# Windowed attention and a gated FFN on one core: queries and keys of steps 4 to 7 in other tiles, and a remade order

## The chip, the core and the metric

The kernel runs on one NeuronCore of a Trainium2 chip. Its engines are TensorE (PE: matmuls; PEld is its weight load), VectorE (DVE), ScalarE (ACT), GpSimd (POOL) and SyncE (SP, which issues the DMAs). The metric is the device time of one execution in microseconds (us).

## The reference

The inputs are q, k and v of 4 batches, 8 heads, 768 tokens and 64 features, 8 memory tokens per head, and the weights of an FFN (512 to 1024 to 512) that come in float64. All heads of one token, side by side, are a row of 512 numbers.

```
for each chunk c of 32 tokens:                       # 24 chunks
    k_full = concat(mem_k, k[16 before .. 8 after])  # 8 + 56 rows
    v_full = concat(mem_v, v[the same])
    a = softmax(q_c @ k_full.T / 8)
    out[c] = a @ v_full
x = out, heads side by side                          # 4 x 768 x 512
h = relu(x @ w_in)                                   # 4 x 768 x 1024
conv = w0 * h[t-1] + w1 * h[t] + w2 * h[t+1]         # per feature, zeros outside
result = (h * sigmoid(conv)) @ w_out                 # 4 x 768 x 512
```

## The kernel before

**Steps of attention.** There are 32 steps, eight to a batch (NU = 8): two halves of 384 tokens (`hf`), in each four pairs of heads (`cc`). A step loads a tile of queries `q_d` (128x768), of keys `k_t` (128x504) and of values `v_t` (128x768), 384, 252 and 384 KB. Its work, with the names that the profile shows:

- the scores `s` (L481), 12 small matmuls of half-size tiles, which the profile counts as 24;
- softmax without the division: the row maximum `top` (L397, DVE), then by the step's letter in `SOFT` either a subtraction on DVE (L402) and one exponential on ACT (L435), or six to seven exponentials on ACT (L423); the row sum `z` (L448), a tiny addition to it (L452, DVE or POOL by `ZADD`), its reciprocal (L455), and the normalisation of `e` (L459, DVE or POOL by `NORM`);
- three transposes `t` (L502), copied to `a_d` by ACT (L513);
- the values' product `a` (L521), 12 small matmuls of half-size tiles, counted as 24;
- the result as two parts whose sum is exact: `x_hi` (L530, ACT) and `x_lo` (L533, DVE).

**FFN.** Each product of the FFN is three matmuls, hi by hi, hi by lo and lo by hi, which the prediction calls a group. The first (L556) makes a tile `f` of 128 features by 384 tokens from four values of `cc`; relu (L573) writes it to `h`. A gate is a first tap (L583 on ACT, L587 on DVE, by `TAP`), two more taps (L593, DVE), a sigmoid (L597) and a product (L601, DVE or POOL, by `MULT`), then a split in two parts (L611 ACT, L614 DVE or POOL, by `LO`). The second product (L632) goes to the output by `o_sb` (L644, ACT) and a DMA. The weights are read as float64 words, 512 KB a piece, eight pieces for each product, and turned into hi and lo in `from_f64` (L286 to L363), with a choice of engines for each piece by a letter of `W_IN` and `W_OUT`. PSUM has two banks for `s`, one each for `t` and `a`, and four for `f`.

**What sets the order.** Nothing runs where it is written. Each operation is given to a `Plan` with an engine, a cost, a due time and its tiles, and `Plan.run` then emits all of them: on each engine it picks among those that could start first the one with the lowest due time. The due times are straight lines in the table `DUE` (start, slope). A matmul operation names a mode, half tiles ("tiled") or whole ones ("whole"), and a change of mode has a cost in the plan. The order that comes out is fixed for each engine when the program is built; on the chip an engine waits at its next instruction until its inputs are there. All loads go through one queue of SP, in order.

**Where the changed tiles lie.** Steps 0 to 3 have queries and keys in the eight tiles of `h`, later used for the relu outputs of batches 1 to 3; all other steps share two `q_d` and two `k_t`. The ring `g` of 16 tiles holds the relu outputs of batch 0 and then the gated splits.

Of the kernel before, what the change touches and what calls it, by code (L numbers as in the profile page):

```python
# [19 lines left out]
CH, LEFT, RIGHT, NMEM = 32, 16, 8, 8  # L20
# [3 lines left out]
NC = 12  # L24
NG = NC // 4
KC = STEP * (NC - 1) + KW
# [3 lines left out]
WC = 512  # L30


W_IN, W_OUT = "CRScCmcc", "McCCMcmm"

TAP = "AAAAAAAAAAAAAAVVAAAAAAAAAVVVVAAA"
MULT = "VVVGGGGGGVGGGGGGGGVGGVGVVGGGGVVV"
LO = "VGVVVVVGGVVVVVGGVVVGGGGVVVGGVVVV"
SOFT = "VVAVVVVVVVABABAAAVVVVVABBBVVAVAB"  # L40
NORM = "GGGGGGGGVVGGGGGGGGGGGGGGVGVVVGVV"
ZADD = "VGGGGVGGGGGVGGVGGVVVVGGGVGGVVVVV"
GROUP = "11111111"

DUE = {
    "early": (1.3, 2.83), "qk0": (-13.5, 0.8), "v0": (104.5, 0), "late": (-19.1, 0), "w_in": (-14.7, 2.93),
    "w_in_load": (-18.2, 4.91), "w_out": (78.5, 2.37), "w_out_load": (4.1, 15.21), "load": (-130.9, 0),
# [4 lines left out]
    "gate": (29.9, 2.03)  # L52
}


# [7 lines left out]
class Plan:  # L63
# [47 lines left out]
    def run(self):  # L111
        ops = self.ops
        n = len(ops)
# [21 lines left out]
        for _ in range(n):  # L135
            best = None
            for e, c in cand.items():
# [20 lines left out]
                if not at:  # L158
                    continue
                t0 = min(at)[0]  # L160
                i = min(
                    (ops[i][2] + (SWITCH if ops[i][7] and ops[i][7] != table else 0) + (MODE if ops[i][8] and ops[i][8] != mode else 0), i)
                    for t, i in at
                    if t <= t0 + 1
                )[1]
# [4 lines left out]
            t, e, i = best  # L170
            eng, cost, due, do, after, tiles, shared, tab, md, late = ops[i]
# [1 line left out]
                cost += 1283  # L173
                table = tab
            if md and md != mode:
                cost += 95 if md == "tiled" else 120
                mode = md
            if e == "DMA":
                queue_free = max(queue_free, t + 600) + cost
# [31 lines left out]


PAIRS = False
SWITCH, MODE = 100.2, 12.1


@with_exitstack
def attention_then_gated_ffn(
# [15 lines left out]
    P = 128  # L234
    NCC, NFC = DM // P, DFF // P
# [9 lines left out]
    def tile_of(tag, n, shape, dtype=F32, pool=None):  # L245

        plan.ring(tag, n)
        pool = pool or work
        return Tile(tag, lambda: pool.tile(shape, dtype, name=tag, tag=tag, bufs=n))

    def bank(tag, n):
        return tile_of(tag, n, [P, 512], pool=psum)
# [13 lines left out]
    def lin(name, i):  # L266
        return DUE[name][0] + DUE[name][1] * i
# [104 lines left out]
    def attention(steps, due, soft, norm, zadd):  # L372
# [9 lines left out]
        for i, n in enumerate(steps):  # L382
            b, r = divmod(n, NU)
            cc = r % NCC

            q_d, k_t = (tile_of(*(("h", NFC) if n < 4 else (x, 2)), y) for x, y in (("q_d", [P, NC, 2 * CH]), ("k_t", [P, KC])))
            v_of[n] = v_t = tile_of("v_t", 3, [P, NG, 2, 2, D])
            s = bank("s", 2)
            qk, vd = (lin("qk0", n), lin("v0", n)) if n < 4 else (due[i] - DUE["load"][0], due[i] - DUE["load"][0] + DUE["load"][1])
            load(q_d, q[b, hf, cc], qk, "p c q -> p (c q)")  # L390
            load(k_t, k[b, hf, cc], qk)
            load(v_t, v[b, hf, cc], vd, "p g c h d -> p (g c h d)")
# [6 lines left out]
            if soft == "V":  # L399
# [3 lines left out]
                        out=part(e, i), in0=s_(), in1=part(top, i).unsqueeze(2).broadcast_to([P, 2 * NG, KW]), op=ALU.subtract  # L403
                    ), (s, (top, i)), ((e, i),),
                )
            else:
# [3 lines left out]
                        out=part(top, i), in0=part(top, i), scalar1=-SCALE, scalar2=None, op0=ALU.mult  # L410
# [21 lines left out]
        due = due[-1]  # L432
# [23 lines left out]
        for i, n in enumerate(steps):  # L456
# [3 lines left out]
                    out=part(e, i), in0=part(e, i), in1=part(z, i).unsqueeze(2).broadcast_to([P, 2 * NG, KW]), op=ALU.mult  # L460
# [4 lines left out]
    def load(tile, src, due, flat=None):  # L465
        size = 1
        for x in src.shape:
            size *= x
        plan.op(
            "DMA", size * 4 / 400, due,  # L470
            lambda: nc.sync.dma_start(out=tile.t.rearrange(flat) if flat else tile.t, in_=src), w=(tile,),
        )
# [196 lines left out]
    def steps(i, n):  # L669

        while i < n:
            size = GROUP[i // 4] == "2" and i % 2 == 0 and 2 or 1
            attention(range(i, i + size), T_ATT[i : i + size], SOFT[i], NORM[i], ZADD[i])
            i += size

    def through_gate(b, fc, due, keep=False):
        i = b * NFC + fc
        return gate(fc, hs[b, fc][0], due, TAP[i], MULT[i], keep)

# [10 lines left out]
    g = []  # L690
    for fc in range(NFC):
        due = lin("gate0", fc)
        g.append(split(*through_gate(0, fc, due), due, LO[fc]))
    for fc in range(NFC):
# [5 lines left out]
    y = [through_gate(1, fc, lin("gate1", fc), True) for fc in range(NFC)]  # L700
    g = [split(*y[fc], lin("split1", fc), LO[NFC + fc]) for fc in range(NFC)]
    steps(16, 24)
# [10 lines left out]
    for b in range(2, B):  # L713
        tokens_in(b, (0, 1), t, 4.2)
        g = []
        for fc in range(NFC):
            due = t + lin("gate", fc)
            g.append(split(*through_gate(b, fc, due), due, LO[b * NFC + fc]))
        if b + 1 < B:
# [81 lines left out]
```

## Time and profile before

| | us |
|---|---|
| median of 3 runs | 359.25 |
| lowest and highest run | 357.82, 360.33 |
| the profiled execution, its own time | 359.63 |
| the span of its profile | 357.6 |
| busy PE, DVE, ACT, POOL | 341.4, 244.7, 240.4, 125.2 |

The profile is of one execution. Its span runs from the first instruction to the last; the execution's own time has some 2 us around it. Busy times of PE are modelled at their ends, since matmuls are pipelined; from one start to the next says more. A wait is put down to the event that came last.

### The profile page before, as it was taken

Reading aid. Unit: us, or ns where it says so; the run is one execution under the profiler, and the core shown is the slowest. Engines: PE = TensorE matmul, PEld = TensorE weight load, DVE = VectorE, ACT = ScalarE, POOL = GpSimd, SP = SyncE. Lnnn points to the kernel's source line nnn. Section 1 sums busy time; section 2 is a strip of 40 time slices with the busy share of each in tenths; the row PEclk is TensorE's granted clock in tenths of the full one; section 3 lists DMA queues with packets and bytes.
Section 4 is the critical chain, followed back from the end, with each engine's and each line's share of the span. In section 5 each row is a group of like instructions: output and inputs, shape, how many; then the busy total and the mean of one; then the engine's idle time right before and its main releaser. Section 6 shows DMA issues by size and latency. Waiting matters only on the chain.

```text
span 357.6 us, 7589 instructions
## 1 busy us (share of the span) xinstructions
PE 341.4 (95%) x3000; PEld 302.1 (84%) x3000; DVE 244.7 (68%) x408; ACT 240.4 (67%) x492; POOL 125.2 (35%) x167
## 2 busy tenths in 40 slices
PE   1699999999999999999999999999999999999996
PEld 1588899999899987778888899997878799998886
DVE  3899898988889998779933026889644128998000
ACT  4468588878679999887979158877466345675101
POOL 2376554442373253774572003354010002560000
PEclk9989999999999999999999999999999999999999
DMA  7999961969623146134416200006272000000111
GB/s 267 402 387 311 383 234 63 341 208 283 209 95 116 25 139 227 68 104 152 129 44 250 88 31 0 2 0 188 80 294 75 30 31 2 0 0 3 59 59 61
DMA packets 19909, 48.63 MB, mean 136 GB/s; under 512 B 2337, under 2 KB 6689, under 8 KB 19873
## 3 DMA queue, kind: packets, MB, share of 16 engines
q1 hardware_dynamic: 19872, 48.14, 39.0%
q8 instruction: 24, 0.39, 0.5%
q14 instruction: 13, 0.10, 0.1%
HBM read 41.84 MB, written 6.29 MB: 135 GB/s over the span
## 4 chain that ended last, share of the span: by engine, by line
PE 69%; DVE 10%; DMA 5%; ACT 5%; POOL 5%; issue 4%; SPq 1%; POOLq 0%; DVEq 0%; ACTq 0%
PE f L632 33%; PE f L556 24%; PE a L521 5%; PE s L481 5%; DVE c L593 3%; PE t L502 2%; DMA h<-in_k_dram 2%; POOL c L601 2%; DMA w<-in_w_out_dram 2%; ACT c L597 2%; DMA w<-in_w_in_dram 2%; POOL w_top L293 2%; DVE z L448 1%; DVE w_top L299 1%; DVE top L397 1%
## 5 line engine op out<-in xcount | busy, mean ns | idle before, releaser
L632 PE MATMUL f<-w_out_hi,g 128*128 128x512 f32 (+1 forms) x400 | 127.6, 391 | 0.2 <-ACT o_sb L644 0.2
L556 PE MATMUL f<-x_hi,w_in_hi 128*128 128x384 f32 x256 | 88.7, 346 | 0.0
L632 PEld LDWEIGHTS f<-w_out_hi,g 128*128 128x128 f32 x400 | 74.1, 188 | 16.3 <-ACT o_sb L644 0.4
L556 PE MATMUL f<-x_hi,w_in_lo 128*128 128x384 f32 x256 | 86.2, 337 | 0.1
L556 PE MATMUL f<-x_lo,w_in_hi 128*128 128x384 f32 x256 | 86.1, 336 | 0.0
L593 DVE SCALAR_TENSOR_TENSOR c<-h,cw,c 128x768 f32<-128x768 f32 x48 | 65.9, 1380 | 27.6 <-ACT c L583 26.1
L632 PE MATMUL f<-w_out_lo,g 128*128 128x512 f32 (+1 forms) x200 | 77.0, 385 | 0.0
L556 PEld LDWEIGHTS f<-x_hi,w_in_hi 128*128 128x128 f32 x256 | 48.1, 188 | 1.2
L556 PEld LDWEIGHTS f<-x_hi,w_in_lo 128*128 128x128 f32 x256 | 48.2, 188 | 0.5 <-POOL w_in_lo L358 0.4
L556 PEld LDWEIGHTS f<-x_lo,w_in_hi 128*128 128x128 f32 x256 | 48.1, 188 | 0.0
L632 PEld LDWEIGHTS f<-w_out_lo,g 128*128 128x128 f32 x200 | 37.6, 188 | 7.2
L601 POOL TENSOR_TENSOR c<-c,h 128x768 f32<-128x768 f32 x9 | 15.8, 1752 | 70.2 <-ACT c L597 68.1
L459 POOL TENSOR_TENSOR e<-e,z 128x384 f32<-128x384 f32 x24 | 24.9, 1035 | 41.4 <-DVE z L455 27.1
L644 ACT COPY o_sb<-f 128x512 f32<-128x512 f32 (+1 forms) x25 | 14.1, 569 | 35.1 <-PE f L632 32.8
L573 ACT ACTIVATE h<-f 128x384 f32<-128x384 f32 x48 | 23.1, 492 | 17.2 <-PE f L556 16.8
L521 PEld LDWEIGHTS a<-a_d,v_t 128*64 128x64 f32 x768 | 25.7, 140 | 10.3 <-issue 5.0
L513 ACT COPY a_d<-t 64x384 f32<-64x384 f32 x64 | 30.3, 474 | 4.3 <-PE t L502 3.3
L533 DVE TENSOR_TENSOR x_lo<-a,x_hi 128x384 fp32r<-128x384 f32 x32 | 17.6, 551 | 22.3 <-ACT x_hi L530 22.2
L521 PE MATMUL a<-a_d,v_t 128*64 128x64 f32 x768 | 29.9, 229 | 1.9 <-ACT a_d L513 1.8
L597 ACT ACTIVATE c<-c 128x768 f32<-128x768 f32 x32 | 26.9, 845 | 3.8 <-DVE c L593 3.6
L530 ACT CAST x_hi<-a 128x384 fp32r<-128x384 f32 x32 | 15.4, 481 | 20.2 <-PE a L521 18.6
L423 ACT ACTIVATE e<-s,top 128x64 f32<-128x64 f32 (+3 forms) x96 | 24.4, 319 | 4.2 <-DVE top L409 2.8
(73 smaller groups left out, 479.8 us busy)
## 6 DMA issues: line engine op xcount, KB each, us to landing
v_t<-in_v_dram SPq DMA_DIRECT2D x32, 384.0 KB, 4.1
q_d<-in_q_dram SPq DMA_DIRECT2D x28, 384.0 KB, 5.1
k_t<-in_k_dram SPq DMA_DIRECT2D x28, 252.0 KB, 5.2
out_dram<-o_sb SPq DMA_DIRECT2D x23, 256.0 KB, 2.1
w<-in_w_in_dram SPq DMA_DIRECT2D x8, 512.0 KB, 5.9
w<-in_w_out_dram SPq DMA_DIRECT2D x8, 512.0 KB, 6.4
h<-in_q_dram SPq DMA_DIRECT2D x4, 384.0 KB, 7.0
h<-in_k_dram SPq DMA_DIRECT2D x4, 252.0 KB, 7.1
```

The costliest lines, as they stand in the source:

```text
L423: nc.scalar.activation(part(e, i)[r, g, c], s_()[r, g, c], AF.Exp, bias=part(top, i)[r, g : g + 1], scale=SCALE, accum_out=part(z, i)[r, g ...
L459: lambda i=i: (nc.vector if norm == "V" else nc.gpsimd).tensor_tensor(out=part(e, i), in0=part(e, i), in1=part(z, i).unsqueeze(2).broadcas ...
L481: nc.tensor.matmul(s.t[j * D : (j + 1) * D, o : o + KW], lhsT=q_d.t[:, c], rhs=k_t.t[:, c * STEP : c * STEP + KW], start=True, stop=True,)
L513: nc.scalar.copy(out=a_d[r, :, p, :], in_=t.t[r, : NG * P].rearrange("p (g q) -> p g q", q=CH))
L521: nc.tensor.matmul(a.t[h * D : (h + 1) * D, g * P + j * D : g * P + (j + 1) * D], lhsT=v_t.t[:, g, j, h], rhs=a_d[:, 4 * g + 2 * j + h].re ...
L533: lambda: nc.vector.tensor_tensor(out=x_lo.t[:, cc], in0=a.t[:, :TW], in1=x_hi.t[:, cc].bitcast(F32), op=ALU.subtract),
L556: nc.tensor.matmul(f.t[:, :TW], lhsT=w_in_p[c][:, fc, cc], rhs=x_p[a].t[:, cc], start=(cc == 0 and i == 0), stop=(cc == NCC - 1 and i == 2),)
L573: nc.scalar.activation(h.t[:, 1 + o : 1 + o + TW], f.t[:, :TW], AF.Relu)
L593: lambda i=i: nc.vector.scalar_tensor_tensor(out=c.t, in0=h.t[:, i : i + S], scalar=w[i], in1=c.t, op0=ALU.mult, op1=ALU.add), (*H, c), (c ...
L597: plan.op("A", act(S), due, lambda: nc.scalar.activation(c.t, c.t, AF.Sigmoid), (c,), (c,), table="sigmoid")
L601: lambda: (nc.vector if mult == "V" else nc.gpsimd).tensor_tensor(out=y(), in0=c.t, in1=h.t[:, 1 : S + 1], op=ALU.mult), (c, h), (h if kee ...
L632: nc.tensor.matmul(ps.t[:, :n], lhsT=g[fc][a].t[:, tt * P : (tt + 1) * P], rhs=w_out_p[c][:, fc, o : o + n], start=(fc == 0 and i == 0), s ...
```

## The change

Queries and keys of steps 4 to 7 go into tiles of the ring `g` (16 tiles) instead of the two `q_d` and two `k_t`, and their loads, and those of the values of these steps, get due times of the lines `qk0` and `v0`, as steps 0 to 3 have. In the plan the change from half tiles to whole ones is counted as 200 ns instead of 120. The tables of due times, of engines (`TAP`, `MULT`, `LO`, `SOFT`, `NORM`, `ZADD`) and of the weights' splits are other ones, and so is the order on every engine.

```diff
-W_IN, W_OUT = "CRScCmcc", "McCCMcmm"
+W_IN, W_OUT = "CRRcCmcS", "ScMMSMRS"
...
-NORM = "GGGGGGGGVVGGGGGGGGGGGGGGVGVVVGVV"
+NORM = "GGGGVGGGVVGGGGGGVVGVGGGVVVVVVVVV"
...
-    "early": (1.3, 2.83), "qk0": (-13.5, 0.8), "v0": (104.5, 0), "late": (-19.1, 0), "w_in": (-14.7, 2.93),
+    "early": (1.3, 2.45), "qk0": (-13.5, 0.48), "v0": (45, 1.91), "late": (-0.2, 2.08),
...
-                cost += 95 if md == "tiled" else 120
+                cost += 95 if md == "tiled" else 200
...
-SWITCH, MODE = 100.2, 12.1
+SWITCH, MODE = 110.1, 13.1
...
-            q_d, k_t = (tile_of(*(("h", NFC) if n < 4 else (x, 2)), y) for x, y in (("q_d", [P, NC, 2 * CH]), ("k_t", [P, KC])))
+            q_d, k_t = (tile_of(*(("h", NFC) if n < 4 else ("g", 2 * NFC) if n < 8 else (x, 2)), y) for x, y in (("q_d", [P, NC, 2 * CH]), ("k_t", [P, KC])))
...
-            qk, vd = (lin("qk0", n), lin("v0", n)) if n < 4 else (due[i] - DUE["load"][0], due[i] - DUE["load"][0] + DUE["load"][1])
+            qk, vd = (lin("qk0", n), lin("v0", n)) if n < 8 else (due[i] - DUE["load"][0], due[i] - DUE["load"][0] + DUE["load"][1])
```

Three places of the order. First the queue of SP behind the last key of step 3 (h_98), before the change; w64 is a piece of weights, v_t_104 the values of step 0, q_d_110 and k_t_112 step 4:

```order
L471 DMA h_98<-in_k_dram 128x504
L286 DMA w64_100<-in_w_in_dram 128x1024
L286 DMA w64_102<-in_conv_w_dram 128x48
L471 DMA v_t_104<-in_v_dram 128x768
L471 DMA v_t_106<-in_v_dram 128x768
L471 DMA v_t_108<-in_v_dram 128x768
L471 DMA q_d_110<-in_q_dram 128x768
L471 DMA k_t_112<-in_k_dram 128x504
```

And now, where g_100 to g_114 are queries and keys of steps 4 to 7 and v_t_120 the values of step 0:

```order
L471 DMA h_98<-in_k_dram 128x504
L471 DMA g_100<-in_q_dram 128x768
L471 DMA g_102<-in_k_dram 128x504
L471 DMA g_104<-in_q_dram 128x768
L471 DMA g_106<-in_k_dram 128x504
L471 DMA g_108<-in_q_dram 128x768
L471 DMA g_110<-in_k_dram 128x504
L471 DMA g_112<-in_q_dram 128x768
L471 DMA g_114<-in_k_dram 128x504
L286 DMA w64_116<-in_w_in_dram 128x1024
L286 DMA w64_118<-in_conv_w_dram 128x48
L471 DMA v_t_120<-in_v_dram 128x768
```

Eight transfers moved ahead of the third piece of w_in, the small conv_w and the first values.

Second, PE from the scores of step 3 (h_98, h_96) on, before:

```order
L481 MATMUL s_195<-h_98,h_96 64x64 x12
L502 MATMUL t_211<-ident_66,e_146 128x128 x3
L521 MATMUL a_240<-a_d_71,v_t_104 64x64 x12
L502 MATMUL t_260<-ident_66,e_170 128x128 x3
L481 MATMUL s_275<-k_t_112,q_d_110 64x64 x12
L521 MATMUL a_292<-a_d_71,v_t_106 64x64 x12
L502 MATMUL t_312<-ident_66,e_217 128x128 x3
L556 MATMUL f_321<-x_hi0_264,w_in_hi_73 128x384
L556 MATMUL f_321<-x_hi0_264,w_in_lo_74 128x384
L556 MATMUL f_321<-x_lo0_273,w_in_hi_73 128x384
L481 MATMUL s_328<-k_t_116,q_d_114 64x64 x12
```

And now:

```order
L481 MATMUL s_211<-h_98,h_96 64x64 x12
L502 MATMUL t_227<-ident_66,e_162 128x128 x3
L481 MATMUL s_249<-g_102,g_100 64x64 x12
L481 MATMUL s_266<-g_106,g_104 64x64 x12
L502 MATMUL t_283<-ident_66,e_186 128x128 x3
L481 MATMUL s_300<-g_110,g_108 64x64 x12
L521 MATMUL a_327<-a_d_71,v_t_120 64x64 x12
L502 MATMUL t_352<-ident_66,e_233 128x128 x3
L556 MATMUL f_359<-x_hi0_343,w_in_hi_73 128x384
L556 MATMUL f_359<-x_hi0_343,w_in_lo_74 128x384
L556 MATMUL f_359<-x_lo0_350,w_in_hi_73 128x384
L521 MATMUL a_365<-a_d_71,v_t_122 64x64 x12
```

The scores of steps 4, 5 and 6 moved ahead of the first values' product, and the second values' product behind the first group of the FFN. Over the whole program PE has 36 stretches of half tiles where it had 37.

Third, DVE around the first x_lo, before (w_100 is the third piece of w_in):

```order
L441 MEMSET e 64x16
L448 TENSOR_REDUCE z<-e 128x6
L293 TENSOR_SCALAR w_top<-w_top 128x512
L533 TENSOR_TENSOR x_lo_273<-a,x_hi_264 128x384
L299 TENSOR_SCALAR w_top<-w_top 128x512
```

And now (w_116 is that piece; the reciprocal and the normalisation are of step 4):

```order
L397 TENSOR_REDUCE top<-s 128x6
L293 TENSOR_SCALAR w_top<-w_top 128x512
L299 TENSOR_SCALAR w_top<-w_top 128x512
L455 RECIPROCAL z<-z 128x6
L459 TENSOR_TENSOR e<-e,z 128x384
L306 SCALAR_TENSOR_TENSOR w_top<-w_116,w_top 128x512
L533 TENSOR_TENSOR x_lo_350<-a,x_hi_343 128x384
```

The first x_lo stands behind more of the softmax of steps 4 to 6 and behind step 4's normalisation, which POOL did before. On POOL the order is the same up to the addition L452 that this reciprocal waits for.

More of the change, by code (lines that the diff above doesn't have):

```diff
@@ L30 @@
 WC = 512
-W_IN, W_OUT = "CRScCmcc", "McCCMcmm"
[L37 to L40, printed above, removed]
-NORM = "GGGGGGGGVVGGGGGGGGGGGGGGVGVVVGVV"
-ZADD = "VGGGGVGGGGGVGGVGGVVVVGGGVGGVVVVV"
+W_IN, W_OUT = "CRRcCmcS", "ScMMSMRS"
+TAP = "AAAAAAAAAAAVVVVVVVAAVVAAAAAAAVVA"
+MULT = "GGGGGGGGGGGGGGGGGGVVVVVGGVVGGGGG"
+LO = "VVVGGVVGGVVVVVVVVVGVVVVVVVVVVVVG"
+SOFT = "VVAVVVVVVVVVVVAABBVVVVVVBAAVBVVB"
+NORM = "GGGGVGGGVVGGGGGGVVGVGGGVVVVVVVVV"
+ZADD = "VGGGGVGGGGGVGGGGVVGGGGGGVVGGVVVG"
 GROUP = "11111111"
 DUE = {
-    "early": (1.3, 2.83), "qk0": (-13.5, 0.8), "v0": (104.5, 0), "late": (-19.1, 0), "w_in": (-14.7, 2.93),
-    "w_in_load": (-18.2, 4.91), "w_out": (78.5, 2.37), "w_out_load": (4.1, 15.21), "load": (-130.9, 0),
[4 rows of a table removed]
-    "gate": (29.9, 2.03)
+    "early": (1.3, 2.45), "qk0": (-13.5, 0.48), "v0": (45, 1.91), "late": (-0.2, 2.08),
+    "w_in": (-13.9, 2.29), "w_in_load": (-18.2, 5.11), "w_out": (61.7, 2.25), "w_out_load": (3.8, 18.52),
[4 rows of a table added]
+    "gate": (33.9, 0)
 }
```

8 rows, old and new, of the table DUE are left out of this document.

## The prediction

> **What bounds the kernel now.** I begin with the page's span and its 40 slices, then ask what TensorE (PE) waited for.
>
> ```profile
> span 357.6 us, 7589 instructions
> PE   1699999999999999999999999999999999999996
> DMA  7999961969623146134416200006272000000111
> ```
>
> PE is full from the third slice (18 us) almost to the last; only the first two slices have much room. A digit of 9 may still hide small waits, so the list of all waits of PE comes next (who waited for what: total us, times, longest).
>
> ```profile
> PE s L481 <- DMA h<-in_k_dram: 8.5, 2, 6.8
> PE a L521 <- ACT a_d L513: 1.8, 1, 1.8
> PE t L502 <- POOL h L544: 0.7, 1, 0.7
> PE t L502 <- POOL e L459: 0.5, 1, 0.5
> PE s L481 <- DVE z L448: 0.4, 1, 0.4
> PE t L502 <- DVE z L452: 0.3, 1, 0.3
> PE f L632 <- ACT o_sb L644: 0.2, 1, 0.2
> ```
>
> The sum is 12.4 us. Of it 6.8 is the arrival of the first query and key, whose place in the queue the change leaves alone. All that a better order can win from waits is 12.4 - 6.8 = **5.6 us**, of which 1.7 (0.7 + 0.5 + 0.3 + 0.2) lies after the first 20 us. The matmuls are the same in number and shape before and after. So the kernel is bound by TensorE's own work, and only its start is open.
>
> What limits the start? Three stages of it (stage, PE busy, granted clock, DMA share, GB/s):
>
> ```profile
> 6.70:15.40 8.70, 6.70 (x99) 1.00 1.03 398
> 15.40:18.70 3.30, 1.48 (x29) 1.00 1.04 398
> 18.70:22.20 3.50, 3.10 (x51) 0.51 1.04 398
> ```
>
> The DMA share is at 1: the engines are saturated at 398 GB/s, and whatever is put ahead in the queue pushes everything behind it back by its bytes. VectorE (DVE) is as full, 3.44 of 3.50 us in the same third stage:
>
> ```profile
> 18.70:22.20 3.50, 3.44 (x7) 0.51 1.04 398
> ```
>
> Three things decide the start: the order of the bytes, VectorE's order, and what PE can do meanwhile.
>
> **Part 1, the loads.** Eight more transfers, the queries and keys of steps 4 to 7, now go ahead of the third input weight and of the first three value tiles.
>
> ```profile
> 9.30 0.33 SPq L471 DMA_DIRECT2D v_t<-in_v_dram  x1
> DMA to landing us min/median/max: 6.3/6.3/6.3
> q_d<-in_q_dram SPq DMA_DIRECT2D x28, 384.0 KB, 5.1
> k_t<-in_k_dram SPq DMA_DIRECT2D x28, 252.0 KB, 5.2
> ```
>
> The first value tile was issued at 9.30 and landed 6.3 us later, at 15.6. Four pairs of 384 + 252 KB are 2.60 MB, at 398 GB/s 6.5 us. It now lands at **22.1 us**. It was needed at 17.48 (next rows), so 1.9 of the 6.5 us was slack, and 4.6 is not.
>
> **Part 2, the start of the FFN matmuls.** What PE did in that time before:
>
> ```profile
> 17.48 0.92 PE L521 MATMUL a<-a_d,v_t 128*64 128x64 f32 x24 [1.82 <-ACT a_d L513]
> 19.27 1.55 PE L481 MATMUL s<-k_t,q_d 128*64 128x64 f32 x24 [0.40 <-DVE z L448]
> 22.39 0.42 PE L556 MATMUL f<-x_hi,w_in_hi 128*128 128x384 f32 x1
> 22.82 0.34 PE L556 MATMUL f<-x_lo,w_in_hi 128*128 128x384 f32 x1
> ```
>
> The first FFN group of three (x_hi by w_hi, x_hi by w_lo, x_lo by w_hi) was through by 23.0. After the change the first value product ends at 22.1 + 0.92 = 23.0 and its copy x_hi comes at about 23.5. Then x_lo must be subtracted on VectorE, and there it now stands behind a normalisation of step 4 that has moved to VectorE, whose reciprocal waits for a small addition on POOL. POOL's order up to that addition is the one of before, so I take POOL's times from the trace:
>
> ```profile
> 21.08 1.70 POOL L351 TENSOR_TENSOR w_in_lo<-w_top,w_in_hi 128x512 fp32r<-128x512 f32 x1
> 22.73 0.83 POOL L459 TENSOR_TENSOR e<-e,z 128x384 f32<-128x384 f32 x1
> L452 POOL TENSOR_SCALAR z<-z 128x6 f32<-128x6 f32 x18 | 7.0, 391 | 22.2 <-DVE z L448 12.7 <-ACT e L423 7.2 <-DVE e L441 1.5
> L455 DVE RECIPROCAL z<-z 128x6 f32<-128x6 f32 x32 | 6.0, 187 | 3.5 <-POOL z L452 2.9
> L459 DVE TENSOR_TENSOR e<-e,z 128x384 f32<-128x384 f32 x8 | 4.4, 556 | 0.2
> L306 DVE SCALAR_TENSOR_TENSOR w_top<-w,w_top 128x512 uint32<-128x512 uint32 x16 | 11.0, 690 | 0.4
> L533 DVE TENSOR_TENSOR x_lo<-a,x_hi 128x384 fp32r<-128x384 f32 x32 | 17.6, 551 | 22.3 <-ACT x_hi L530 22.2
> ```
>
> POOL's multiplication ends at 22.73 + 0.83 = 23.56, the addition (0.39) at 23.95. Then on VectorE come the reciprocal 0.19, the normalisation 0.56, the weight step 0.69 and x_lo 0.55: 25.9. The first group is through at about **26.2** instead of 23.0.
>
> Queued behind it on PE, which works in order, are the second value product and the scores of step 7. Ahead of it stand the scores of steps 4 to 6, which the early loads allow. So I count what PE had done by 26.3 (rows of the scores, the transposes, the value products and the FFN groups; 24, 3, 24 and 3 instructions make one):
>
> ```profile
> 0.00:26.30 26.30, 8.66 (x144) 7.73 (x144) 0.94 0.95 353
> 0.00:26.30 26.30, 2.39 (x12) 1.57 (x12) 0.94 0.95 353
> 0.00:26.30 26.30, 3.36 (x72) 3.00 (x72) 0.94 0.95 353
> 0.00:26.30 26.30, 2.02 (x8) 1.41 (x9) 0.94 0.95 353
> ```
>
> Before: 6 scores, 4 transposes, 3 value products, 3 groups (the ninth matmul just starting). After, by the times above: 7, 3, 1 and 1. The prices come from a dense stretch, and that of three transposes from the chain of waits:
>
> ```profile
> 35.35 0.34 PE L556 MATMUL f<-x_hi,w_in_lo 128*128 128x384 f32 x1
> 35.52 0.34 PE L556 MATMUL f<-x_lo,w_in_hi 128*128 128x384 f32 x1
> 35.81 0.92 PE L481 MATMUL s<-k_t,q_d 128*64 128x64 f32 x24
> 36.54 0.89 PE L521 MATMUL a<-a_d,v_t 128*64 128x64 f32 x24
> 37.36 0.44 PE L556 MATMUL f<-x_hi,w_in_hi 128*128 128x384 f32 x1
> 37.64 0.33 PE L556 MATMUL f<-x_hi,w_in_lo 128*128 128x384 f32 x1
> 58.50 0.33 PE t L502 x3
> ```
>
> From start to start a whole matmul takes 0.17, so a group 0.52. The scores take 0.73 to the next start; I use 0.75 for them and for a value product, and 0.33 for the transposes. Two value products (1.50), two groups (1.04) and a transpose (0.33) less, one score (0.75) more: PE is 2.1 us of work behind. It has also gone into half tiles only 3 times, not 5. Such a round trip costs 0.29 - 0.17 on the way in, 0.82 - 0.75 on the way out, and 0.28 - 0.17 at the second whole matmul: **0.3 us**. Two of them are still unpaid, 0.6. So the start costs 2.7 us. From there to 52 us I find both orders equally dense, but for a VectorE step of the fourth input weight, which stands ahead of other work and lands later: 0.1 more, an estimate by the same steps. I take **+2.8**. The ends: -0.3, if x_lo came as soon as x_hi is there, at 24.1 (PE would then have eight scores done and be a little ahead); +4.6, the whole delay of the first value tile. The addition on POOL is a measured time, so I stay near the middle.
>
> One row speaks against the change beyond this. In the stage from 18.7 to 22.2 the clock granted was 0.51, and the scores took 1.55 instead of 0.92. [...]
>
> **Part 3, the changes of tile size.** The planner now counts a change to whole tiles at 200 instead of 120 ns, a number that runs nowhere on the chip. PE's order has 36 stretches of half tiles against 37: one round trip, **-0.3 us** (bounds -0.6 and 0, twice the price or none).
>
> **Part 4, the moved work behind the start.** Softmax, normalisation, gating and weight splitting change engines, and their loads with them. All of it lies beside PE, which waited 1.7 us after 20 us. These waits can go (-1.7), or as many can come (+1.7, the nearest rows being those waits). With no row that tells which of them stay, I take **-0.5**, a little under a third of them, for ACT has fewer instructions now. If the cover were gone in one place, the longest of these waits, 0.7, is what one such miss cost.
>
> Sum: 357.6 + 2.8 - 0.3 - 0.5 = 359.6 us of span. The profiled execution took 359.63 for its 357.6, so 2.0 lies around it: **361.6 us**. That is 0.7% above the median of 359.25, whose runs reach from 357.82 to 360.33; 1% (3.6 us) is about what a measurement here can tell from no change.
>
> **The rivals.**
>
> *The start costs nothing.* For it: the early scores fill PE, and POOL's addition may come earlier than the mean says. Against it: 22.73 + 0.83 is measured, not modelled. Then 361.6 - 2.8 = **358.8**.
>
> *The clock falls once more* (slower, the other side). Between 22.1 and 25.9 PE has one value product, transposes and two thirds of a group to do, some 0.92 + 0.33 + 0.35 = 1.6 of 3.8 us, as thin as the 1.48 of 3.30 that stood ahead of the clock of 0.51. If 3.5 us at half clock follow, half of them, 1.7 us, is lost: 361.6 + 1.7 = **363.3**, 1.1% above the median. [...] Against it: PE waits there anyway, so part of a slow stage may cost nothing.
>
> *All the waits go* (faster). If the remade order closes every wait but the first: 359.63 - 5.6 - 0.3 = **353.7**. For it: every engine's order was changed. Against it: 2.2 of the 5.6 stands in the first 20 us as waits for values' path and softmax, which now have their bytes later, not sooner; and 1.7 more is the second key, whose place has not moved.
>
> **How the numbers follow.** Chances: the forecast 0.50, the start for nothing 0.17, the clock 0.25, all waits gone 0.08. Low end: the forecast with its terms at their good ends, 359.63 - 0.3 - 0.3 - 1.7 = 357.3, which takes in 358.8. High end: the clock's case with 4.6 instead of 2.8 at the start, 365.1. Left out are the case of 0.08 and the rest of the tails. Faster by over 1% (under 355.7) is the last rival alone: 0.08. Slower by over 1% (above 362.8): 0.18 of the clock's 0.25, and 0.06 of the forecast's 0.50, where the start costs over 4: 0.24. Within 1%: 0.68.
>
> **What would show it.** Right: the first value tile lands near 22; the first FFN group runs at 25.5 to 26.5; by 26.3 PE has 7 scores and 1 value product; PE's waits in the first 30 us sum to more than before, after that to under 2 us; the dense stretch at the end is as long as now. Wrong: a first group before 24.5 (then the start term is too big); a stage after 22 us with a clock near 0.5 (the second rival); or new waits of over 1 us each in the middle, for weights of the second FFN step or for a gate, which no row of before lets me place.

## The result, and the profile after

Twelve executions of the changed kernel took a median of **362.01 us** (360.18 to 363.39), twelve of the kernel before beside them 360.08 us (357.82 to 362.36). The ratio is **1.0064**, with a 95% interval of 1.0043 to 1.0086: about 2.3 us slower. The forecast was 361.6 us in a range of 357.3 to 365.1. The profiled execution took 360.43 us for a span of 358.6.

The page first, with the span, PE's 40 slices and the granted clock (the share of TensorE's full rate that the profile records, in tenths):

```profile
span 358.6 us, 7535 instructions
PE   1579999999999999999999999999999999999996
PEclk9989999999999999999999999999999999999999
```

PE's second and third digits were 6 and 9 and are 5 and 7: what was lost stands in the first 27 us. The waits of PE say for whom (us in total, times, longest):

```profile
PE s L481 <- DMA h<-in_k_dram: 9.4, 2, 7.7
PE t L502 <- issue: 1.5, 1, 1.5
PE s L481 <- ACT e L423: 1.2, 1, 1.2
PE s L481 <- DVE e L402: 0.6, 1, 0.6
PE t L502 <- DVE e L459: 0.6, 2, 0.4
PE t L502 <- POOL e L459: 0.6, 1, 0.6
PE a L521 <- DMA v_t<-in_v_dram: 0.4, 1, 0.4
```

They sum to 14.3 us, against 12.4; those of the first 30 us to 13.7, where they were 10.7. In the first row 0.9 us is the first key, which landed at 7.6 in this execution and at 6.7 in the profiled one of before. That is not the change: up to that key the queue is the same, and in the other profiles of this study the first matmul starts anywhere from 6.1 to 8.0 us. Of these waits only the fifth, 0.6 us, comes after 30 us. The stages of the start, on the bounds used before (PE busy, granted clock, DMA share, GB/s):

```profile
15.40:18.70 3.30, 1.78 (x27) 0.83 1.04 401
18.70:22.20 3.50, 2.85 (x49) 0.67 1.04 392
22.20:26.00 3.80, 1.89 (x44) 1.00 1.03 396
```

The new thin stage is the third, 1.89 of 3.80 us. PE's timeline shows what it did there:

```profile
23.03 0.92 PE L521 MATMUL a<-a_d,v_t 128*64 128x64 f32 x24 [0.42 <-DMA v_t<-in_v_dram]
25.44 0.52 PE L502 MATMUL t<-ident,e 128*128 128x128 f32 x3 [1.49 <-issue]
25.71 0.42 PE L556 MATMUL f<-x_hi,w_in_hi 128*128 128x384 f32 x1
26.30 0.44 PE L556 MATMUL f<-x_lo,w_in_hi 128*128 128x384 f32 x1
```

The first value product starts at 23.03, the first group of the FFN ends at 26.7; before these were 17.48 and 23.16. POOL's and VectorE's timelines show the x_lo that the third matmul waited for, behind the reciprocal, the normalisation and the weight step:

```profile
23.82 0.29 POOL L452 TENSOR_SCALAR z<-z 128x6 f32<-128x6 f32 x1
23.35 0.67 DVE L293 TENSOR_SCALAR w_top<-w_top 128x512 f32<-128x512 f32 x1
24.05 0.43 DVE L299 TENSOR_SCALAR w_top<-w_top 128x512 uint32<-128x512 uint32 x1
24.40 0.18 DVE L455 RECIPROCAL z<-z 128x6 f32<-128x6 f32 x1
24.61 0.56 DVE L459 TENSOR_TENSOR e<-e,z 128x384 f32<-128x384 f32 x1
25.09 0.68 DVE L306 SCALAR_TENSOR_TENSOR w_top<-w,w_top 128x512 uint32<-128x512 uint32 x1
25.69 0.55 DVE L533 TENSOR_TENSOR x_lo<-a,x_hi 128x384 fp32r<-128x384 f32 x1
```

POOL's addition, which the prediction let release the reciprocal, ended at 24.11 (predicted 23.95). But the reciprocal ran only at 24.40, behind two other weight steps: VectorE had been busy without a real pause since 21.1 us. So here VectorE's own order set x_lo, not POOL.

And one hold that the prediction did not have. The transposes at 25.44 waited 1.49 us for "issue", which names no event. ACT's timeline names it:

```profile
23.99 0.48 ACT L530 CAST x_hi<-a 128x384 fp32r<-128x384 f32 x1 [0.59 <-PE a L521]
24.37 0.97 ACT L513 COPY a_d<-t 64x384 f32<-64x384 f32 x2
```

There is one bank for `t` and one `a_d`. The bank is read by the copies to `a_d` that end at 25.34, those copies must wait until the first value product has read the old `a_d`, and on ACT they stand behind x_hi. So the transposes, and the FFN group queued behind them on PE, wait for the same late value tile by a second way.

### The profile page after: what moved, and what is told of

The parts are those of the page before. It is cut to its first block, busy times and chain, and to the rows that moved or that the text cites. A ratio compares the mean times of both kernels' runs of the same rounds, so it can differ in the third digit from the quotient of the medians.

```text
span 358.6 us, 7535 instructions
## 1 busy us (share of the span) xinstructions
PE 340.7 (95%) x3000; PEld 301.5 (84%) x3000; DVE 252.5 (70%) x414; ACT 228.0 (64%) x450; POOL 123.8 (35%) x167
## 4 chain that ended last, share of the span: by engine, by line
PE 79%; DVE 9%; DMA 6%; ACT 2%; POOL 1%; issue 1%; SPq 0%; ACTq 0%
PE f L632 34%; PE f L556 31%; PE a L521 6%; PE s L481 4%; PE t L502 3%; DVE c L593 2%; DMA g<-in_q_dram 2%; DMA w<-in_w_in_dram 2%; DMA h<-in_k_dram 2%; DVE e L459 1%; DVE w_top L299 1%; DVE w L327 1%; DVE g L614 1%; DMA k_t<-in_k_dram 1%; DVE w_top L306 1%
## 5 line engine op out<-in xcount | busy, mean ns | idle before, releaser
L556 PE MATMUL f<-x_hi,w_in_hi 128*128 128x384 f32 x256 | 88.9, 347 | 0.0
L556 PE MATMUL f<-x_lo,w_in_hi 128*128 128x384 f32 x256 | 86.2, 337 | 0.0
L556 PE MATMUL f<-x_hi,w_in_lo 128*128 128x384 f32 x256 | 86.1, 336 | 0.0
L593 DVE SCALAR_TENSOR_TENSOR c<-h,cw,c 128x768 f32<-128x768 f32 x48 | 59.8, 1247 | 8.8 <-ACT c L583 7.5
L556 PEld LDWEIGHTS f<-x_hi,w_in_hi 128*128 128x128 f32 x256 | 48.1, 188 | 1.3
L556 PEld LDWEIGHTS f<-x_lo,w_in_hi 128*128 128x128 f32 x256 | 48.1, 188 | 0.3 <-DVE x_lo L533 0.3
L556 PEld LDWEIGHTS f<-x_hi,w_in_lo 128*128 128x128 f32 x256 | 48.2, 188 | 0.0
L533 DVE TENSOR_TENSOR x_lo<-a,x_hi 128x384 fp32r<-128x384 f32 x32 | 17.6, 549 | 16.4 <-ACT x_hi L530 16.3
L611 ACT CAST g<-c 128x768 fp32r<-128x768 f32 x24 | 20.0, 832 | 12.3 <-POOL c L601 8.0
L530 ACT CAST x_hi<-a 128x384 fp32r<-128x384 f32 x32 | 15.4, 480 | 15.6 <-PE a L521 15.2
L587 DVE TENSOR_SCALAR c<-h,cw 128x768 f32<-128x768 f32 x11 | 9.5, 866 | 21.3 <-ACT h L573 21.3
```

Of the source, the lines that this page charges most:

```text
L530: plan.op("A", act(TW, True), due, lambda: nc.scalar.copy(out=x_hi.t[:, cc], in_=a.t[:, :TW]), (a,), ((x_hi, cc),))
L533: lambda: nc.vector.tensor_tensor(out=x_lo.t[:, cc], in0=a.t[:, :TW], in1=x_hi.t[:, cc].bitcast(F32), op=ALU.subtract),
L556: nc.tensor.matmul(f.t[:, :TW], lhsT=w_in_p[c][:, fc, cc], rhs=x_p[a].t[:, cc], start=(cc == 0 and i == 0), stop=(cc == NCC - 1 and i == 2),)
L593: lambda i=i: nc.vector.scalar_tensor_tensor(out=c.t, in0=h.t[:, i : i + S], scalar=w[i], in1=c.t, op0=ALU.mult, op1=ALU.add), (*H, c), (c ...
L611: plan.op("A", act(S), due, lambda: nc.scalar.copy(out=g_hi(), in_=x()), (h,), (p[0],))
```

## The experiments

Times of before stand beside each, from the same chip. "Idle by 36 us" is the time to 36 us, less what the matmuls done by then take in a dense stretch (0.173 us a matmul of 384, 0.73 a set of scores, from start to start) and less 0.3 us a round trip of tile size. What a half clock costs counts as idle in it. It is 16.0 us in the profile of before and 18.5 in that of after.

### One part taken back, or done alone

The first four take the change apart by its edits and let the planner make a new order.

The old tiles and loads of steps 4 to 7, with all the new tables:

```diff
-            q_d, k_t = (tile_of(*(("h", NFC) if n < 4 else ("g", 2 * NFC) if n < 8 else (x, 2)), y) ...
+            q_d, k_t = (tile_of(*(("h", NFC) if n < 4 else (x, 2)), y) ...
...
-            qk, vd = (lin("qk0", n), lin("v0", n)) if n < 8 else ...
+            qk, vd = (lin("qk0", n), lin("v0", n)) if n < 4 else ...
```

> The changed kernel with queries and keys of steps 4 to 7 back in the two shared tiles and their loads at the old kind of due time; the new tables and the new cost of a change stay, and the planner makes the order anew (39 stretches of half tiles; before 37, changed 36). Theory START (the loss is the start: values 6.5 us later in the queue, then x_lo late): values land near 15.6 again, the first FFN group is done near 23, the time goes back to that of before plus two round trips of 0.3 us, less some 1 us of later waits: ratio to before 0.997 to 1.003. Rival LATER (the loss is in the remade tables, behind the start): the ratio stays at 1.005 to 1.009.

Measured: 364.52 us, ratio 1.0127 (1.0072 to 1.0182), 39 stretches of half tiles. Idle by 36 us went back to 16.3, so the start was won back. But the waits of PE after 36 us grew to 4.6 us (0.6 in after), in seven places, the longest 1.1 us. The total lies above both expected ranges, with an interval that reaches into that of the rival: with these tables and without the new placement, the planner's order is worse behind the start.

The new tiles and loads alone, in the kernel before (the same two lines the other way round):

> The kernel before with one part alone: queries and keys of steps 4 to 7 in the ring g and the loads' due times by the lines qk0 and v0; old tables, old cost. The planner gives 43 stretches of half tiles (before 37), and queries and keys of steps 4 to 6 stand ahead of the third input weight and the values. START: the start costs 2 to 3 us and six round trips 1.8 us, sum 4 to 5 us, ratio 1.011 to 1.014. Rival (the place itself costs nothing, the remade tables do): only the round trips, ratio about 1.005.

Measured: 366.55 us, 1.0160 (1.0104 to 1.0217). Idle by 36 us is 19.6, 3.6 more than before, with the value tile late again and six round trips more. The first of these waits is the value tile at the start; the other two come between 110 and 124 us:

```profile
PE a L521 <- DMA v_t<-in_v_dram: 1.8, 1, 1.8
PE s L481 <- DVE e L441: 1.4, 1, 1.4
PE f L556 <- ACT h L573: 1.0, 1, 1.0
```

The ratio is a little above what START expected, with that range inside the interval, and the rival's 1.005 is out. So the early loads cost the start about the same with the old tables as with the new (3.6 us against 2.5 and, in a second profile below, 3.8), and the kernel that has the tables and the cost of the change too is the faster one (1.0064 against 1.0160).

The 200 ns for a change of tile size alone:

```diff
-                cost += 95 if md == "tiled" else 120
+                cost += 95 if md == "tiled" else 200
```

> The kernel before with the other part alone: the change from half to whole tiles counted as 200 instead of 120 ns in the plan. 39 stretches of half tiles against 37. START: the head of the queue is that of before, so the start costs nothing, and two round trips cost 0.6 us: ratio 1.000 to 1.004. Rival (a truer cost makes a better order by itself): ratio 0.994 to 0.998.

Measured: 361.62 us, 1.0024 (0.9996 to 1.0053); idle by 36 us 17.0. That number by itself does no harm that these runs can tell from none, and no good.

The changed kernel with the first three values due ahead of queries and keys of steps 4 to 7:

```diff
+            qk, vd = (-5 + 0.3 * n if 4 <= n < 8 else qk), (-7 + 0.1 * n if n < 3 else vd)
```

> The changed kernel with one thing other: the first three value tiles are due ahead of the queries and keys of steps 4 to 7 (which stay in the ring g, directly behind them), the planner makes the order anew, 40 stretches of half tiles against 36. START by bytes: the first value tile lands near 14.5, the first FFN group is done by 23, and against the changed kernel 2 to 3 us are won and 1.2 us lost to four round trips: ratio to before 1.000 to 1.004. Rival (the order on VectorE and POOL decides, not the bytes): no gain at the start, ratio 1.008 to 1.011.

Measured: 363.30 us, 1.0092 (1.0063 to 1.0120), 40 stretches. The start came back in full (idle by 36 us 16.1) and the total was worse by more, since the planner remade everything behind it. The total agrees with the rival, its mechanism does not. One line of a due time can't be changed here without changing the whole order, so the next runs fix the order by hand.

### The start alone exchanged, the rest fixed

The operations of after are emitted in after's order, number for number, but the first 200 of them in the order of the run just above, which has the values early. Stretches stay at 36.

```diff
+START = [
+    83, 11, 12, 94, 29, ...
+]
...
+    return START + seq[len(START):]
...
+        self.emit(reorder(self, seq))
```

> The changed kernel with its first 200 planned operations (the first 35 us or so, on all engines) in the order of e4_values_first, and every later operation in the changed kernel's own order, number for number; 36 stretches of half tiles as there. Theory START (the changed kernel's loss is its start alone): PE is 2.0 to 2.5 us less idle up to 36 us than in the changed kernel, waits behind it stay, ratio to before 0.997 to 1.002. Rival CATCH-UP (what is lost at the start would be waited for later anyway, at the input weights or gates): the lead is gone by 75 us, ratio 1.004 to 1.008.

Measured: 360.71 us against 360.11, ratio **0.9997** (0.9971 to 1.0023); after's own is 1.0064 (1.0043 to 1.0086). The intervals do not touch: the loss is in the first 200 operations. PE's timeline of this run, where L569 is the value product and L604 the FFN:

```profile
17.61 1.44 PE L569 MATMUL a<-a_d,v_t 128*64 128x64 f32 x24 [2.03 <-ACT a_d L561]
21.27 0.45 PE L604 MATMUL f<-x_hi,w_in_hi 128*128 128x384 f32 x1
```

The value product stands at 17.6 again, where it was before the change (17.48), the first group 1.1 us ahead of where it was (22.39). Idle by 36 us is 15.6, by 52 us 18.4 (19.1 in after): of 2.9 us that the start won, 2.2 came back as a wait, mostly one of 2.0 us of a value product between 36 and 42 us. Since the first key was 1.3 us earlier than in after's profile, the two numbers are not exactly comparable. The spans of the two profiles differ by 0.8 us only (357.8 and 358.6), the ratios by more: the rest lies in executions that these two profiles do not show, and the part on the clock takes them up.

The same with the first 300, to see whether that wait is the seam of the two orders:

> The order of after the change, but with the first 300 planned operations (instead of 200 in the run before that kept the rest) in the order that takes the first three values ahead of queries and keys of steps 4 to 7; the others keep their order, number for number; 36 stretches of half tiles. In the run with 200 PE was idle 15.6 us by 36 us but 18.4 by 52 us: some 2.2 us of the start's gain were handed back. Theory SEAM: it was handed back because the two orders meet at 200, and an order that goes on longer keeps it: idle time by 52 us under 18.0, end 0.5 to 1 us earlier, ratio to before 0.994 to 0.999. Rival WORK: PE is ahead of the weights and of the softmax that the other engines must do in that stretch whatever the order, so PE's being ahead there can't be kept: idle by 52 us 18 to 19, ratio 0.998 to 1.003, no better than with 200.

Measured: 359.55 us against 359.20, 0.9992 (0.9967 to 1.0018). Idle by 52 us is 18.9 where the first key was 1.2 us later than with 200; the 2.0 us wait is gone, 0.8 and 0.5 us for weights stand in its place. The seam was part of it, and the time does not show it: both ratios agree with the rival as well. It is the best order of the study, and level with before.

### The price of a round trip

After's order with 14 more round trips: behind the first 60 operations of PE, where two half-tile operations follow one another, the second goes behind the next whole one.

```diff
+        if k > 60 and k + 2 < len(p) and mode[k] == mode[k + 1] == "tiled" and mode[k + 2] == "whole":
+            new += [p[k], p[k + 2], p[k + 1]]
```

> The changed kernel's order with one thing other: where two half-tile operations stand side by side on PE behind the first 60, the second goes behind the next whole-tile operation. 50 stretches of half tiles instead of 36; nothing else moves. If a round trip costs 0.3 us, 14 more cost 4.2 us: ratio to before 1.015 to 1.021. Rival (a round trip is hidden among the pipelined matmuls): ratio 1.005 to 1.009. Rival (as the plan counted it before, 95 + 120 ns): 3.0 us, ratio about 1.014 to 1.016.

Measured: 368.14 us, 1.0202 (1.0141 to 1.0264), 1.4% over after's ratio, as expected. Compared at one level of the clock (next part) its executions are 5.2 us above those of after (368.23 and 363.06 us in the mean); 1.1 of it is a wait for a gate that only its profile has. Fourteen trips are worth 4.1 to 5.2 us, **0.29 to 0.37 us** each. The two kernels were timed on different chips, and the ratio's interval alone would leave room for the planner's old price of 0.215. The profiles do not: from 52 us to the end, where the record shows full clock in both, this run's idle time with the trips is 5.4 us more than after's for 15 more trips, 1.1 of it that wait. That leaves 0.29 us a trip.

### The two holds ahead of the first group

The first value tile ahead of the query and key of step 7 in SP's queue, all else as in after:

```diff
+    new = q[:16] + [q[20], q[18], q[19], q[16], q[17]] + q[21:]
```

> The changed kernel's order with one thing other, on the DMA queue: the first value tile goes ahead of queries and keys of step 7, the second and third keep their places. The first value tile lands 3.1 us sooner, near 19 to 20. If the bytes ahead of the values decide the first FFN group alone, it is done 1 us or more sooner than in the changed kernel (26.5). If x_lo behind POOL's addition decides as well, as the prediction has it, x_lo still starts at 25.5 to 25.9 and the first group is done at most 0.2 us sooner.

Profiled once: 361.24 us. The value tile landed at 19.3 instead of 23.0, the value product ran at 20.59, and still (L556 is the transposes here, L610 the FFN):

```profile
23.83 0.52 PE L556 MATMUL t<-ident,e 128*128 128x128 f32 x3 [2.37 <-POOL z L506]
25.69 0.44 PE L610 MATMUL f<-x_lo,w_in_hi 128*128 128x384 f32 x1 [0.99 <-DVE x_lo L587]
```

The third matmul, by x_lo, is 0.6 us earlier than in after, for a value product 2.4 us earlier (the first key was 0.5 us earlier too). That lies between the two expected numbers. VectorE's order held it: x_lo stood behind the reciprocal at 23.79, and that behind a weight step (to 23.66) and POOL's addition (to 23.75) at nearly the same time, as the prediction had it. The transposes' row names POOL's addition too, but ACT's copies out of the bank of `t` ended at 23.73 as well.

The same, with x_lo also ahead of reciprocal, normalisation and weight step on VectorE:

```diff
+    return after_op(seq, d[39:42], d[42])
```

> As e7_value_sooner, and on VectorE the first x_lo goes ahead of the reciprocal and normalisation of step 4 and the weight step. With both holds gone the first FFN group is done 0.6 to 0.9 us sooner than in the changed kernel (26.5 there). Rival (a third hold, such as POOL or ACT, takes the place): less than 0.3 us.

Profiled once: 361.34 us. VectorE did x_lo at 23.88 instead of 25.09, but (L563 is the transposes, L617 the FFN)

```profile
24.81 0.52 PE L563 MATMUL t<-ident,e 128*128 128x128 f32 x3 [3.41 <-issue]
25.70 0.53 PE L617 MATMUL f<-x_lo,w_in_hi 128*128 128x384 f32 x1
```

and nothing was won over the run before. ACT's timeline shows what came late instead:

```profile
22.12 0.66 ACT L350 ACTIVATE w_top<-w 128x512 f32<-128x512 f32 x1 [1.26 <-DMA w<-in_w_in_dram]
22.68 0.66 ACT L393 ACTIVATE w<-w 128x512 f32<-128x512 uint32 x1
23.37 0.48 ACT L591 CAST x_hi<-a 128x384 fp32r<-128x384 f32 x1
23.74 0.97 ACT L574 COPY a_d<-t 64x384 f32<-64x384 f32 x2
```

The value product was done by 21.5, but x_hi and the copies that free the bank of `t` stand behind two steps of the third input weight, whose bytes landed only at 22.1. In the run before, from the same place in the queue, they landed at 21.1, so 1.0 us of this is that execution, and one profile of each can't say what x_lo ahead wins by itself. Against after the first group ended 0.6 us earlier in the run before and 0.5 us earlier in this one. It hangs on three queues at once, SP's, VectorE's and ACT's; what all three freed would give was not tried.

### The clock

The profile of after had no second fall of the clock. But each timed execution has its mean granted clock, by the profiler's record (which begins at 14.2 us in after's profile, see the end), and they have levels. In the profiles 3.41 us of half clock stand beside a mean of 0.995 (after), 6.83 us beside 0.990 (the run with the first 300 exchanged) and 10.24 us beside 0.986 (the run with more round trips); I read the means of the timed executions by that as one, two or three such stretches. Of the twelve executions of after, five stood at 0.986 and took 363.0 us in the mean, five at 0.995 and took 360.9. The run with more round trips was profiled at 0.986, and the first 60 operations of its PE are after's. Its stages of 3.4 us:

```profile
18.20:21.62 3.42, 0.92 (x24) 1.00 1.04 393
21.62:25.03 3.41, 1.54 (x24) 0.50 1.03 397
25.03:28.44 3.41, 2.21 (x14) 0.50 1.04 400
28.44:31.86 3.42, 3.42 (x49) 0.50 0.70 248
```

There the first key came at 6.1, the scores were done sooner, and PE stood idle for 3.2 us ahead of the value tile. The half clock then lasted for 10.2 us, into the dense stretch. Does that happen in after, and does PE's being idle make it? After once more, unchanged:

> The kernel after the change, unchanged, beside the kernel before on one chip, with the mean granted clock of every execution. In its profile the half clock lasted 3.5 us (mean granted clock 0.995), but 5 of its 12 timed executions had 0.986, and took 2.1 us longer in the mean (363.0 to 360.9); the run with 14 more round trips, which has the same order up to 24 us, was profiled with 0.986 and shows half clock from 21.8 to 31 us. Theory CLOCK: in some executions of this order the half clock stays for two or three stretches of 3.3 us instead of one, since PE stands idle ahead of the first value product: 30 to 60 in 100 executions at 0.986, at most 10 in 100 of the kernel before (whose profile has no such gap); those of 0.986 take 1.5 to 2.5 us longer than those of 0.995. Rival CHANCE: the levels of the clock come as often in both kernels, and the 5 of 12 were luck: the shares differ by under 20 in 100. Either way the ratio is 1.004 to 1.009.

Measured: 362.41 us against 359.66, ratio 1.0069 (1.0038 to 1.0100). Mean granted clocks and times:

| mean granted clock | after, 12 executions | before, 29 executions |
|---|---|---|
| 0.986 | 5, mean 363.1 us | none |
| 0.989 to 0.991 | 4, mean 362.2 us | 6, mean 361.9 us |
| 0.993 to 0.998 | 3, mean 361.6 us | 23, mean 359.4 us |

Chance is out: over both runs of after, 10 of 24 executions stand at 0.986, none of these 29 of before, and of 51 timed beside the earlier runs one, at 0.984. The mean clock is not all, though: the three of these 51 at 0.999 or 1.000 took 360.3 to 361.8 us, above the medians of 360.0 and 360.1 beside which they stood. The profiled one had one half-clock stretch, at a worse place than before the change (from 25.1 us on, where the FFN's matmuls are dense; before the change it lay from 18.8 to 22.2):

```profile
22.20:25.50 3.30, 0.92 (x25) 0.94 1.03 395
25.50:28.80 3.30, 3.30 (x38) 0.54 1.03 402
```

Then after with 60 small matmuls more, which nothing reads, ahead of the first value product:

```diff
         def values():
+            for g in [0, 1, 2] * (5 if n == 0 else 0):
+                ...   # scores of step 0 again, into a, overwritten below
```

> After the change, the order unchanged, with 60 small matmuls more (half tiles of step 0's keys and queries, overwritten afterwards) ahead of the first value product, where PE stands idle for up to 3.2 us. They add no result and cost 60 x 31 ns = 1.9 us of PE at full clock, all of it beside the wait for the first value tile when the first key comes early, 1.4 us of it uncovered when it comes late. Theory CLOCK: PE is then busy there, so the half clock does not stay: executions at 0.986 fall from some 40 to under 15 in 100, median 360.5 to 362, ratio 1.001 to 1.006, up to 1 us below the kernel without the filling. Rival CHANCE: the clock does not follow from PE's being idle there: the share of 0.986 stays over 25 in 100 and the median is 0 to 1.5 us above the kernel without it, ratio 1.006 to 1.011.

Measured, beside the run above: **361.20 us**, ratio to before 1.0040 (1.0010 to 1.0070). Eleven of twelve executions have a clock of 1.000, the twelfth 0.999. PE's timeline (L526 is the filling; the profile counts its 60 matmuls as 120):

```profile
20.50 3.72 PE L526 MATMUL a<-h 128*64 128x64 f32 x120
24.00 0.92 PE L536 MATMUL a<-a_d,v_t 128*64 128x64 f32 x24
27.11 0.34 PE L571 MATMUL f<-x_lo,w_in_hi 128*128 128x384 f32 x1
```

The filling took 3.7 us, twice the 1.9 that was expected: 12 such matmuls take 0.73 us, 61 ns each and not 31. So it ran into the value product's place, and the third matmul of the first group is 0.3 to 0.8 us later than in the two profiles of after. Still the kernel is 1.07 us faster in the mean (361.34 to 362.41 over twelve each, ratio 0.9970, bootstrap interval 0.9958 to 0.9984). Useless work on PE made it faster, and the clock is what it kept:

```profile
18.70:22.20 3.50, 2.60 (x85) 1.00 1.03 391
22.20:25.50 3.30, 2.72 (x93) 1.00 1.04 396
```

Last, 48 such matmuls (2.9 us of PE, again twice what was expected) in the run with the other 300 operations, which had 6.8 us of half clock in its profile:

> The order with the first values early (first 300 planned operations), with 48 small matmuls more (1.5 us of PE, overwritten afterwards) ahead of the first value product at 15.9 to 17.9 us, where PE stands idle for 2.0 us. In the profile without them a half clock of 6.4 us follows from 17.7 on. Theory CLOCK: PE busy there keeps the clock up or shortens the half clock to one stretch: mean granted clock 0.995 or more in over 80 in 100 executions (6 to 7 of 12 without), time 0.3 to 2 us lower, ratio to before 0.994 to 0.998. Rival CHANCE: the clock's levels stay as they are (a third or more of the executions at 0.990 or below), ratio 0.998 to 1.002.

Measured: 359.88 us, 1.0005 (0.9976 to 1.0034). The clock's part held, 11 of 12 executions at 0.998 or more and none under 0.995; the time's part missed, for it is no faster than without (0.9992). Without the filling the half clock lay from 17.4 to 24.2 us. With it PE was 2.4 us ahead by 24 us (idle time and filling together 14.6 us, against 17.0; 1.1 of it is a first key that came earlier), and by 30 us it had given that back as waits (17.3 against 17.1): one value product alone waited 1.5 us, and this profile has a half clock of its own from 28.0 us on. The likely reading, by these two profiles, is that a faster PE there only waits for the other engines, while in after the half clock reached into the dense part, where PE sets the pace.

## Why the prediction was right, and where it was not

**The loads.** The first value tile landed at 23.0 (predicted 22.1). From the last key of step 3 to it, 2.4 us passed before and 8.9 after: the 6.5 us for the bytes were right. But the landing was not an effect of one late first key. In the four profiles with this queue it was 22.8 to 23.2, though the first matmul started at 6.1 and 6.2 us in two of them and at 7.7 and 8.0 in the others. So the forecast was 0.7 to 1.1 us early, and a late first key only shortens the wait for the value tile (3.2 us with the key at 6.1 us, 0.4 and 1.7 with it at 7.7 and 8.0).

**The start of the FFN.** x_lo ran from 25.69 to 26.24 (predicted to end at 25.9), the first group at 25.7 to 26.7 (predicted through at 26.2). What PE had done by 26.3 was predicted as 7 sets of scores, 3 of transposes, 1 value product and 1 group, and is, in the rows of the four:

```profile
0.00:26.30 26.30, 9.22 (x168) 8.31 (x168) 5.98 (x11) 1.34 (x6) 0.94 0.93 352
0.00:26.30 26.30, 1.97 (x9) 1.12 (x9) 1.90 (x4) 0.94 0.93 352
0.00:26.30 26.30, 0.92 (x24) 0.78 (x24) 0.55 (x1) 0.48 (x1) 0.94 0.93 352
0.00:26.30 26.30, 0.58 (x3) 0.31 (x3) 0.94 0.93 352
```

168 small matmuls are seven sets of scores, nine are three sets of transposes, 24 one value product, three one group. The term of +2.8 us measures, by idle time to 36 us, +2.5 in the first profile of after and +3.8 in the second (idle by 36 us 19.8), which holds a half clock in the dense part. The exchanged start shows the place. That VectorE was a hold is shown by the value tile sent ahead; what stood ahead of the reciprocal in after was VectorE's own weight steps, with POOL's addition, the prediction's measured time, 0.3 us before their end. That ACT's queue was a second hold, at nearly the same time, the prediction had missed, without an effect on the sum.

**Tile size.** 0.3 us a round trip agrees with 0.29 to 0.37. The one trip fewer can't be seen in a total.

**Later waits** were mis-sized. PE's idle time from 36 us to the end is 2.6 us before (18.6 less 16.0) and 1.5 in both profiles of after: -1.1, not -0.5. The waits after 20 us that were 1.7 in before are 0.6 after 30 us now, so two thirds went instead of a third.

Sum by the profiles: +2.5 or +3.8, less 0.3, less 1.1, is +1.1 or +2.4; the spans of 358.6 and 360.0 against 357.6 are +1.0 and +2.4.

**The rivals.** *The start costs nothing* fell: exchanging the start alone took the loss away. *All the waits go* fell. *The clock falls once more* was put as another world, with a chance of 0.25 and a time of 363.3. It is a part of this one: the longer half clock comes in some executions and not in others. In 10 of 24 there are three half-clock stretches, by their mean clock, and these took 363.0 and 363.1 us in the mean; those at 0.995 took 360.9 and 361.6. The median lies between, so that it came within half a microsecond of 361.6 is luck in part: more of the later waits went than forecast, which makes the executions with one half-clock stretch faster than 361.6, and three stretches, which the forecast did not have, make others slower. The step that failed is the forecast's clock, taken as that of one profiled execution. The filling, which took away all the half clock that the record shows in after's start, won 1.1 of the 2.5 us that lay between the means of after and before (362.41 and 359.90). The profiled execution of after, at 0.995, would have passed for proof that the rival was wrong; the clocks of the timed executions showed it.

**What stays open.** At 0.995 before is still some 2 us faster than after (359.4 and 361.6 in the table). That lies at the start; how it splits between the queues of SP, VectorE and ACT was not settled, since behind each one that was freed the next held, in one profile of each.

## What to carry to other kernels

At a start that is bound by the DMA queue (here a DMA share of 1.03 to 1.04 at 392 to 401 GB/s), what is loaded ahead is paid for by whatever lands behind it (here 2.60 MB, and the first value tile at 23.0 instead of 15.6 us): ask what the matrix engine's first long chain needs (here the first values, through ACT and VectorE), and put that ahead of work that merely fills. Look at an idle gap of the matrix engine not only for its length but for the clock that it leaves behind (in the run with more round trips 3.2 us of idle PE, and 10.2 us of half clock that began in it), and read the granted clock of every timed execution, not of the profile alone; in one of the two orders tried here, 60 matmuls that nothing reads were cheaper than the gap, by 1.07 us in the mean. To judge one part of a planner's order, fix the order of the rest: two of the four edits that let the planner run again cost 4 to 5 us of idle time behind the start, against after.

## What the hardware did that was not expected

At the start of two executions of one order the half clock began at different times: at 17.6 us in the profile of after and at 25.1 in that of after once more, and lasted 3.41 us in both, as in before (from 18.8 us on). It lasted longer elsewhere: in the run with the first 300 exchanged 6.83 us, from 17.4 on; in the one with more round trips 10.24 us, from 21.6 on. The order with the first 300 exchanged shows what PE did around it:

```profile
13.97:17.38 3.41, 1.35 (x27) 1.00 1.04 393
17.38:20.79 3.41, 2.85 (x37) 0.50 1.04 391
20.79:24.21 3.42, 3.42 (x36) 0.50 1.04 396
24.21:27.62 3.41, 3.41 (x88) 1.00 1.04 399
```

1.35 us busy, then half clock; 2.85 busy at half clock, and it stays; 3.42, and it is gone. In the 3.41 us ahead of the fall PE was busy 1.59 us in the profiles of before and of after, and 0.92 in those of after once more and of more round trips, so in none of these was it idle throughout: in the second profile of after no single gap of PE there was longer than 1.7 us. Behind a stretch of 1.86 us in the first profile of after, and behind one of 1.88 in the second, the clock stayed full; in the last run it fell at 28.0 us, behind 1.35 and 1.10 us busy in the two stretches of 2.00 us before. At half clock the last stretch had 3.02 us busy in before, 3.41 in after and 3.06 in after once more. How much work keeps the clock, and how much brings it back, these few profiles do not settle.

The record of the clock also has a gap. It begins at 15.4 us in the profile of before and at 14.2 us in that of after, and the rows give 1.00 for what lies ahead of it. But the same 24 small matmuls, from PE's timeline of before:

```profile
6.82 1.55 PE L481 MATMUL s<-h 128*64 128x64 f32 x24 [6.82 <-DMA h<-in_k_dram]
23.09 0.92 PE L481 MATMUL s<-k_t,q_d 128*64 128x64 f32 x24
```

The first set took as long as the one at 19.27 us under a granted clock of 0.51, 1.55 us each. In the profiles of before and of after such a matmul takes 314 ns in the median up to 13 us, and 222 from 30 us on at full clock. So I take PE to have run at half rate up to there, an estimate from these times, before the change as after it, and the 1.00 in the prediction's row from 6.70 to 15.40 us is the gap, not the clock. Nor do the mean clocks of the executions hold this stretch: the 0.995 of after's profile is what 3.41 us at half clock take from its 358.6 us.
